# Blocks 3 and 4 of the tokens as a third pair with seven products of sums, on one core

## The chip, the core and the metric

The kernel runs on one core of a Trainium2 chip. Its engines are TensorE (PE, with weight loads as PEld), VectorE (DVE), ScalarE (ACT), GpSimd (POOL) and SyncE (SP), which here issues all the DMAs. The metric is device microseconds of one execution; the kernel before took a median of 988.34 us in three runs (987.86 to 989.14).

## The reference

Attention of 8 batches, 8 heads, 576 queries and head size 64, with keys and values averaged over groups of 8 positions (72 remain), and then a gated network with normalised rows on all 4608 tokens:

```python
k_p = k.reshape(B, H, Sp, pool, D).mean(axis=3)
v_p = v.reshape(B, H, Sp, pool, D).mean(axis=3)
scores = scale * np.matmul(q, k_p.transpose(0, 1, 3, 2))
attn = np.exp(scores - scores.max(-1)); attn = attn / (attn.sum(-1) + 1e-09)
x = np.matmul(attn, v_p)                      # to (4608, 512)
xn = x / np.sqrt(np.mean(x * x, -1) + 1e-06) * rms_g
g = xn @ w_gate                               # (512, 1536)
out = (g / (1 + np.exp(-g)) * (xn @ w_val)) @ w_out   # (1536, 512)
```

(Reductions keep their axis in the reference.) The weights arrive as float64 and are used as a high and a low fp32r half.

## The kernel before

**Blocks.** The 4608 tokens are nine blocks of 512. Each product of two fp32 operands is made as three fp32r matmuls (high by high, low by high, high by low). A block on its own ("plain") needs for each of the 12 column groups f of the hidden layer 12 matmuls for the gate and 12 for the value (`mm1`, L1016, into `psg`) and 12 for the output (`mm2`, L1050, into `po`): 432 in all. Blocks 0 to 4 are plain. Blocks 5 and 6, and blocks 7 and 8, are pairs: a pair is treated as a 2 by 2 block matrix that is multiplied with seven products instead of eight, in layer 1 (`product`, L852, into `pxy`, 12 x 7 x 6 = 504 matmuls) and in layer 2 (`product2`, L932, into `pf`, 7 x 6 x 6 = 252): 756 for two blocks.

**What a pair needs.** Sums of blocks of the weights: `w_whole` (high plus low, L712 on POOL or L714 on DVE, tile `wsum`), `w_sum` (L723, four sums for each f), `w_sumhi` (ACT, L728) and `w_sumlo` (L732, tile `wt`), for layer 2 `v_whole`, `v_sum`, `v_sumhi`, `v_sumlo` (L759, L763, L767). They are made while the plain blocks run and are stored to DRAM (`w_store`, `v_store`, and `w_blocks`, `v_blocks` for the unsummed parts), and in a pair each product loads its 256 KB back (`w_part` into `wp`, `f_part` into `ring`). Sums of the tokens (`p_sum`, `p_hi`, `p_lo`) are made just ahead of a pair. In a pair DVE and ACT combine the seven products (L1110 to L1119), and the sums of the hidden layer are formed on DVE and POOL (`f_sum`, `f_lo`, all through the helper `cut`, L272).

**Start.** The weights are split into halves by ACT, DVE and POOL (`w_abs` L298, `w_shift` L302, `w_low` L306, `w_sign` L310, `w_hi` L324, `w_lo` through L272) in the prelude and in block 0. The attention of batches 0 and 1 takes the `_` steps (`s_max`, `s_exp`, `s_inverse`, `s_norm`); that of batches 2 to 7 the `l_` steps. Attention has to be ahead of the block that uses its tokens: pair 5 and 6 uses batches 4 to 7.

**The order.** The string `ORDER` is a list of steps written by a planner and played back; nothing reorders it later. Each engine runs its instructions in that order and waits at each for its inputs. In a step's name the letters are the operation, the digits its indices (`mg1a` is the gate product of block 1, f = 10); figures behind `:` are PSUM banks and behind `/` buffer slots. SP's DMAs stand in one queue in the same order.

Of the kernel before, what the change touches and what calls it, by code (L numbers as in the profile page):

```python
# [57 lines left out]
_a0/0 _S10:24 _l7/0 _A030:6 _C032 _b0 _a2 _h1 _y01 _x00 _M100 _N010 _T010:5 _l4 _T012:7 _c0 _d0 _y00 _P00:3 _a4 _b4
_Z20 _M101 _D010 _x20 _A010:5 _h0 _E100 _y20 _E101 _C012 _W1 _A031:1 _A011 _A021:2 _x21 _Z31 _W0 _m000:7 _b2 _m010:4
_Z11 _c2 _x11 _X021 _d2 _R101 _y21 _m002 _R100 _x30 _c4 _d4 _m012 _k11 _Z10 _P01 _N101 _x10 _Z21 _h2 _l3/1 _y30 _N100  # L60
_T100:2/0 _y11 _x31 _a3/0 _b3 _q11 _Y011 _y10 _c3 _Z30 _P02 _P03 _m011 _W2 _l6 _a6 _m001 _h4 _V10/0 _p _r0 _m110:6
_y31 _m013 _b6 _T101 _d3 _T102:5 _s0 _c6 _l8 _a8 _B00:3 _d6 _Y031 _m003 _D100 _la _b8 _D101 _n _h6 _a7/1 _m100:1 _m112
_l9/1 _u0 _W4 _D102 _m102 _m111 _m101 _A100:5/1 _G0 _c8 _Y100 _K11/1 _d8 _S11:20 _m103 _W6 _F0 _i0/1 _M110 _h3 _aa _W3
_j0 _u1 _m113 _g2:3 _M111 _G1 _a9/0 _h8 _F1 _o0:6475 _W8 _i1/0 _E110 _L1 _b9 _E111 _c9 _d9 _e2:1 _h9 _W9 _ba _ca _da
_ha _b7 _e4:2 _c7 _q12 _k12 _o1 _d7 _lc _ac _Wa _u2 _bc _g3:3 _K12/1 _G2 _h7 _W7 _F2 _i2/1 _e3:0 _L2 _cc _dc _lb/1
_ld/0 _ab/0 _o2 _bb _u3 _le _g4:3 wd3 _ae _G3 _cb _R110 _N110 _R111 _v11 _ad/1 _F3 _i3/0 _be _hc _L3 _db _hb _o3
# [1097 lines left out]
```

## Time and profile before

| | |
|---|---|
| median of three runs | 988.34 us |
| the profiled execution | 985.33 us |
| its span, first to last instruction | 983.2 us |
| PE busy | 962.6 us (98%) |
| DVE / ACT / POOL busy | 665.9 / 477.1 / 446.8 us |
| moved by DMA | 178.37 MB, 181 GB/s |

The profiled execution is 3.0 us below the median and 2.1 us above its own span. A busy time is a union: an instruction counts until its end. A matmul's row gives the time from its start to its modelled end, and the next one starts well before that end, so the pace of PE is read from runs of matmuls in the chain and not from a mean. Borders between the blocks are the starts of their first `psg` or `pxy` matmul: block 0 at 40.1 us, then 166.8, 281.9, 397.1, 506.6 (block 4), 617.4 (first pair) and 780.4 (second pair).

### The profile page before, as it was taken

How to read it: one execution, taken by the hardware profiler on the slowest of the kernel's cores; microseconds unless marked ns; L12 is line 12 of the kernel's file. 1: busy time of each engine (PE TensorE's matmuls, PEld its weight loads, DVE VectorE, ACT ScalarE, POOL GpSimd, SP SyncE). 2: the span in 40 equal slices, each digit the busy share in tenths (PEclk: the TensorE clock that was granted, in tenths of full speed). 3: DMA queues.
4: the chain of work that ended last, by engine and by line, in shares of the span. 5: the costliest groups of instructions: out<-in, count | busy, mean ns of one | idle time of the engine just before them, and what ended most of it. 6: DMA issues, size and time to landing. Idle time of an engine off the chain costs nothing.

```text
span 983.2 us, 14009 instructions
## 1 busy us (share of the span) xinstructions
PE 962.6 (98%) x4778; PEld 768.7 (78%) x4778; DVE 665.9 (68%) x1043; ACT 477.1 (49%) x936; POOL 446.8 (45%) x535
## 2 busy tenths in 40 slices
PE   6899999999999999999999999999999999999997
PEld 6687878777877878778777778888787778888885
DVE  5997988666776576777686756665666885445343
ACT  6885776454554534743464254533434651222232
POOL 1688773223432543524453133323437762135567
PEclk7799999999999999999999999999999999999999
DMA  8546566466466444585435523776586565666546
GB/s 268 200 169 191 190 187 207 118 198 186 128 214 181 123 144 120 157 250 166 138 123 170 150 93 88 235 237 206 182 267 219 178 213 183 213 232 209 186 143 196
DMA packets 119542, 178.37 MB, mean 181 GB/s; under 512 B 10224, under 2 KB 67056, under 8 KB 118192
## 3 DMA queue, kind: packets, MB, share of 16 engines
q1 hardware_dynamic: 119472, 177.48, 57.4%
q8 instruction: 38, 0.62, 0.3%
q14 instruction: 32, 0.26, 0.1%
HBM read 121.21 MB, written 56.23 MB: 180 GB/s over the span
## 4 chain that ended last, share of the span: by engine, by line
PE 86%; DVE 6%; DMA 3%; ACT 2%; POOL 1%; issue 1%; SPq 0%; DVEq 0%; ACTq 0%; POOLq 0%
PE psg L1016 31%; PE pxy L852 23%; PE po L1050 16%; PE pf L932 9%; PE psx L521 3%; PE pss L439 3%; DMA v<-vN 2%; DVE wt L306 1%; DVE wt L310 1%; POOL fp L272 1%; DVE xl L272 1%; DMA ring<-vB 1%; DVE wt L302 1%; DMA ring<-vs 0%; POOL w L272 0%
## 5 line engine op out<-in xcount | busy, mean ns | idle before, releaser
L1016 PE MATMUL psg<-xh,w 128*128 128x512 f32 x928 | 289.4, 393 | 0.0
L852 PE MATMUL pxy<-xp,wp 128*128 128x512 f32 x1008 | 239.8, 390 | 1.5 <-ACT acc L591 1.0
L852 PEld LDWEIGHTS pxy<-xp,wp 128*128 128x128 f32 x1008 | 188.3, 188 | 43.6 <-issue 1.4
L1016 PEld LDWEIGHTS psg<-xh,w 128*128 128x128 f32 x928 | 172.0, 188 | 42.9 <-issue 4.1
L1016 PE MATMUL psg<-xl,w 128*128 128x512 f32 x464 | 181.0, 390 | 0.5 <-DVE xl L272 0.4
L272 POOL TENSOR_TENSOR hl<-act,hh 128x256 fp32r<-128x256 f32 x90 | 74.7, 850 | 160.0 <-ACT hh L1032 126.2
L932 PE MATMUL pf<-fp,ring 128*128 128x512 f32 x504 | 125.4, 391 | 1.5 <-DMA ring<-vB 1.0
L1050 PE MATMUL po<-w,hh 128*128 128x512 f32 x480 | 121.2, 390 | 0.0
L932 PEld LDWEIGHTS pf<-fp,ring 128*128 128x128 f32 x504 | 93.6, 188 | 24.2 <-issue 1.9
L1050 PEld LDWEIGHTS po<-w,hh 128*128 128x128 f32 x480 | 90.1, 188 | 19.0
L1016 PEld LDWEIGHTS psg<-xl,w 128*128 128x128 f32 x464 | 87.1, 188 | 19.9 <-DVE xl L272 1.4
L1028 DVE TENSOR_TENSOR act<-act,psg 128x512 f32<-128x512 f32 x60 | 41.0, 683 | 66.4 <-PE psg L1016 42.9
L272 POOL TENSOR_TENSOR w<-wt,w 128x256 fp32r<-128x256 f32 x68 | 72.3, 1090 | 13.7 <-ACT w L324 9.1
L1032 ACT CAST hh<-act 128x512 fp32r<-128x512 f32 x60 | 37.2, 619 | 74.5 <-DVE act L1028 48.4
L1050 PE MATMUL po<-w,hl 128*128 128x512 f32 x240 | 68.6, 397 | 1.4 <-POOL hl L272 1.4
L1050 PEld LDWEIGHTS po<-w,hl 128*128 128x128 f32 x240 | 43.9, 188 | 12.8 <-POOL hl L272 2.2
L272 POOL TENSOR_TENSOR fp<-fs,fp 128x256 fp32r<-128x256 f32 x54 | 41.2, 788 | 21.8 <-ACT fp L905 21.8
L272 POOL TENSOR_TENSOR fp<-act,fp 128x256 fp32r<-128x256 f32 x34 | 25.3, 764 | 50.5 <-ACT fp L905 49.1
L1023 ACT ACTIVATE act<-psg 128x512 f32<-128x512 f32 x48 | 28.6, 597 | 37.1 <-PE psg L1016 27.3
L1023 ACT ACT_TABLE_LOAD x26 | 33.4, 1283 | 22.3 <-PE psg L1016 15.6
L905 ACT CAST fp<-fs 128x512 fp32r<-128x512 f32 x36 | 21.7, 619 | 41.7 <-PE pf L932 24.9
L439 PEld LDWEIGHTS pss<-pk,q 64*128 64x128 f32 x560 | 33.4, 188 | 10.0 <-issue 7.3
(191 smaller groups left out, 1506.6 us busy)
## 6 DMA issues: line engine op xcount, KB each, us to landing
wp<-sum SPq DMA_DIRECT2D x96, 256.0 KB
wp<-blocks SPq DMA_DIRECT2D x72, 256.0 KB
blocks<-w SPq DMA_DIRECT2D x24, 512.0 KB
sum<-wt SPq DMA_DIRECT2D x48, 256.0 KB
ring<-vs SPq DMA_DIRECT2D x48, 256.0 KB
wx<-w SPq DMA_DIRECT2D x10, 1024.0 KB
v<-vN SPq DMA_DIRECT2D x32, 288.0 KB
ring<-vB SPq DMA_DIRECT2D x36, 256.0 KB
```

Of the source, the lines that this page charges most:

```text
L272: getattr(eng, op)(*(x[..., o:o + step] for x in (out, a, b)))
L302: nc.vector.tensor_scalar(u, u, 3, None, ALU.logical_shift_left)
L439: nc.tensor.matmul(s["ps", h][:, t * SP:(t + 1) * SP], s["q"][r, o:o + P], s["pk"][r, :], start=True, stop=True)
L521: nc.tensor.matmul(ps[r, :n], s["pv"][:, r], x, start=True, stop=True)
L852: nc.tensor.matmul(ps[:, :NB], w[:, a, c, :], x[:, b, c, :], start=j == 0 and not more, stop=j == len(todo) - 1, skip_group_check=more)
L905: nc.scalar.copy(y[:, 0], f_source(i, k, j))
L932: nc.tensor.matmul(ps[c], w[:, a, c * P:(c + 1) * P], x[:, b], start=j == 0 and n == 0 and not more, stop=j == HALF - 1 and n == 2, skip_g ...
L1016: nc.tensor.matmul(ps[:, :NB], w[:, c, cols], x[c], start=(j == 0), stop=(j == len(todo) - 1))
L1023: nc.scalar.activation(t, ps[:, :NB], AF.Silu)
L1028: nc.vector.tensor_mul(t, t, ps[:, :NB])
L1032: nc.scalar.copy(a, st["act", i, f])
L1050: nc.tensor.matmul(po[i][t], x[i, f][:, t * P:(t + 1) * P], w, start=(f == 0 and k == 0), stop=(f == NF - 1 and k == 2))
```

## The change

`FIRST`, the number of plain blocks, falls from 5 to 3, so that blocks 3 and 4 are a pair too. All the sums of the weights and the attention of batches 0 to 4 then have to be ready by the end of block 2. For the prelude there are three new steps: the second heads of batch 0 subtract the maximum on DVE (`s_sub`), take one exponential of 360 columns on ACT in place of five of 72 (`s_expall`), and sum and invert on DVE (`s_suminverse`), for which each row has a 73rd column of 1e-9. The factor 1/8 of the averaged values moves from the sum to the copies of `x`. `ORDER` is another string of 3315 steps (2990 before).

```diff
-FIRST = 5
+FIRST = 3
-            s["main"] = space1(NF - 1 - 2 * p, [P, 2 * S + 10 * SP], F32, f"main{p}")
+            s["main"] = space1(NF - 1 - 2 * p, [P, 2 * S + 10 * (SP + 1)], F32, f"main{p}")
+            nc.gpsimd.memset(rows(p)[:, :, SP:], 1e-9)
...
+    def s_sub(b, p, h):
+        s, n = st[b, p], len(OFFS2)
+        s["pr", h] = pr = s_rows(b, p, h)[:, :, :SP]
+        nc.vector.tensor_tensor(pr, s["ps", h][:, :n * SP].rearrange("p (t k) -> p t k", k=SP),
+                                s["mx"][:, h, :, None].broadcast_to([P, n, SP]), ALU.subtract)
+    def s_expall(b, p, h):
+        pr = st[b, p]["pr", h]
+        nc.scalar.activation(pr, pr, AF.Exp, scale=EXP_SCALE)
+    def s_suminverse(b, p, h):
+        sm = st[b, p]["sm"][:, h, :]
+        nc.vector.tensor_reduce(sm, s_rows(b, p, h), AX.X, ALU.add)
+        nc.vector.reciprocal(sm, sm)
...
-            copy(xraw[b][:, p, s["tok", u]], s["psx", u][:, :S // 2])
+            x, y = xraw[b][:, p, s["tok", u]], s["psx", u][:, :S // 2]
+        if eng is nc.scalar:
+            eng.mul(x, y, 1.0 / POOL)
...
-        if i < FIRST - 1:
+        if i < FIRST:
             t = sb1.tile([P, NC, n], F32, tag="q", name=f"tail{b}")
-        else:
-            t = space1(0, [P, NC, n], F32, f"tail{b}")
+            t = t[:, :2], t[:, 2:]
+        else:
+            t = sb1.tile([P, 2, n], F32, tag="q", name=f"tail{b}_0"), space2(NF - 1, [P, 2, n], F32, f"tail{b}_1")
...
-_l9/1 _u0 _W4 _D102 _m102 _m111 _m101 _A100:5/1 _G0 _c8 _Y100 _K11/1 _d8 _S11:20 _m103 _W6 _F0 _i0/1 _M110 _h3 _aa _W3
+_S11:27 _b9 _C102 _c9 _d9 _M110 _h9 _m102 _E110 _b8 _m110 _m112 _M111 _F0 _w9 _m101 _W6 _c8 _i0/1 _L0 Wf00 _d8 _lb/0
```

The engines' queues before and after show what the new order moves. First DVE in block 0, between the gate multiplications of f = 4 and f = 5 (`act0_4`, `act0_5`; `wt14`, `wt16` are weights being split, `wsum1` and `wt1_4` are sums for the pairs). Before:

```order
L1028 TENSOR_TENSOR act0_4_912<-act0_4_912,psg0_4_1_753 128x512
L306 SCALAR_TENSOR_TENSOR wt13_884<-wx13_838,wt13_884 128x512
L310 SCALAR_TENSOR_TENSOR wt13_884<-wx13_838,wt13_884 128x512
L306 SCALAR_TENSOR_TENSOR wt14_875<-wx7_857,wt14_875 128x1024
L310 SCALAR_TENSOR_TENSOR wt14_875<-wx7_857,wt14_875 128x1024
L404 TENSOR_REDUCE early_86<-pss1_2_0_953 128x5
L404 TENSOR_REDUCE early_86<-pss1_2_1_954 128x5
L990 TENSOR_TENSOR act0_5_1012<-xraw0_299,psg0_5_0_976 128x512
```

In the changed kernel the same stretch of DVE's queue, to the same multiplication (line numbers are those of the changed file):

```order
L1071 TENSOR_TENSOR act0_4_951<-act0_4_951,psg0_4_1_937 128x512
L326 SCALAR_TENSOR_TENSOR wt14_963<-wx7_934,wt14_963 128x1024
L330 SCALAR_TENSOR_TENSOR wt14_963<-wx7_934,wt14_963 128x1024
L419 TENSOR_REDUCE pv2_0_1007<-v2_0_1005 72x128
L757 TENSOR_TENSOR wsum2_1034<-w1_2_576 128x1024
L463 RECIPROCAL early_87<-early_87 128x5
L775 TENSOR_TENSOR wt1_4_1056<-wsum1_959,wt1_4_1056 128x256
L766 TENSOR_TENSOR wsum2_1034<-wsum2_1034 128x2x128
L775 TENSOR_TENSOR wt1_3_1027<-wsum1_959,wt1_3_1027 128x256
L322 TENSOR_SCALAR wt16_1071<-wt16_1071 128x1024
L766 TENSOR_TENSOR wsum2_1034<-wsum2_1034 128x2x128
L1033 TENSOR_TENSOR act0_5_1106<-xraw0_379,psg0_5_0_1043 128x512
```

The splitting of the weights stands where it stood, and the sums for the pairs, of which block 0 had none, now stand between them on DVE. Up to the gate multiplication of block 1, f = 0, DVE has 272 instructions where it had 217.

Second, SP's queue in the middle of the first pair, at the loads of layer 1 for f = 9 (`wp`), of layer 2 (`ring2`), and what belongs to attention (`k`, `q`, `v`, `rows`, `pt`). Before, in the pair of blocks 5 and 6:

```order
L841 DMA wp5_8_6_6887<-blocks8_5275 128x2x256
L920 DMA ring2_5999<-vB21_0_1958 128x512
L841 DMA wp5_9_3_6911<-sum9_3_4867 128x512
L480 DMA rows7_2_6932<-sq7_2_6736 32x3x256 x2
L480 DMA rows7_2_6932<-sq7_2_6736 32x3x320 x2
L485 DMA pt7_2_6937<-rows7_2_6932 72x1152
L841 DMA wp5_9_5_6939<-sum9_1_4921 128x512
L920 DMA ring2_5999<-vs1_2_3107 128x512
L841 DMA wp5_9_4_6951<-sum9_4_4852 128x512
```

In the changed kernel, in the pair of blocks 3 and 4:

```order
L884 DMA wp3_9_4_5440<-sum9_4_3080 128x512
L963 DMA ring2_3429<-vs0_2_1880 128x512
L884 DMA wp3_9_3_5463<-sum9_3_3023 128x512
L884 DMA wp3_10_3_5475<-sum10_3_3390 128x512
L390 DMA q6_3_5489<-qT 128x576
L884 DMA wp3_9_2_5491<-blocks9_3900 128x2x256
L401 DMA v6_3_5503<-vN 72x1024
L963 DMA ring2_3429<-vs1_2_2544 128x512
L884 DMA wp3_10_1_5527<-sum10_2_3291 128x512
L519 DMA rows6_2_5531<-sq6_2_5479 32x3x256 x2
L519 DMA rows6_2_5531<-sq6_2_5479 32x3x320 x2
```

The first pair now carries the attention of batches 5, 6 and the start of 7 in its loads, where before it had the end of batch 7 alone: from the pair's first product to the next pair's, SP issues 174 DMAs where it issued 139.

## Rows read from the trace of the kernel before

**Rows 1.** The page, busy us (share) by engine.

```profile
PE 962.6 (98%) x4778; PEld 768.7 (78%) x4778; DVE 665.9 (68%) x1043; ACT 477.1 (49%) x936; POOL 446.8 (45%) x535
```

**Rows 2.** Windows by block: us, busy PE, PEld, DVE, ACT, POOL, PEclk, DMA, GB/s.

```profile
40.10:166.80 126.70, 124.56 (x651) 100.21 (x650) 110.58 (x147) 91.54 (x196) 95.18 (x92) 0.98 0.56 181
166.80:281.90 115.10, 115.10 (x606) 90.92 (x605) 80.89 (x143) 58.28 (x102) 30.49 (x39) 1.00 0.54 164
617.40:780.40 163.00, 162.04 (x750) 130.29 (x748) 107.04 (x160) 70.02 (x114) 72.68 (x92) 1.00 0.68 217
780.40:983.20 202.80, 195.92 (x852) 158.70 (x852) 105.43 (x143) 61.67 (x105) 101.75 (x128) 1.00 0.62 197
```

**Rows 3.** Chain of waits in order of time: start us, us, what.

```profile
12.25 11.21 DMA v<-vN
78.02 4.27 POOL w L272 x4
...
198.41 8.16 PE psg L1016 x36
331.85 2.75 PE po L1050 x12
830.83 20.40 PE pxy L852 x90
```

**Rows 4.** Grouped instructions of DVE, shapes apart: busy us, mean ns, idle before.

```profile
L732 DVE TENSOR_TENSOR wt<-wsum,wt 128x256 fp32r<-128x256 f32 x30 | 16.5, 558 | 9.2 <-ACT wt L728 9.2
L723 DVE TENSOR_TENSOR wsum<-wsum 128x256 f32<-128x256 f32 x27 | 15.5, 576 | 0.9 <-POOL wsum L723 0.4
L714 DVE TENSOR_TENSOR wsum<-w 128x1024 f32<-128x1024 f32 x7 | 8.8, 1254 | 1.9 <-POOL acc L272 1.9
L272 DVE TENSOR_TENSOR hl<-act,hh 128x512 fp32r<-128x512 f32 x15 | 12.1, 810 | 5.1 <-ACT hh L1032 5.0
L272 DVE TENSOR_TENSOR w<-wt,w 128x1024 fp32r<-128x1024 f32 x1 | 1.2, 1218 | 0.0
L759 DVE TENSOR_TENSOR vsum<-vsum 128x256 f32<-128x256 f32 x16 | 7.8, 487 | 1.6 <-POOL vsum L272 1.3
L456 DVE TENSOR_TENSOR prob<-pss,mx 128x360 f32<-128x360 f32 x48 | 24.5, 524 | 0.7
L464 DVE TENSOR_REDUCE sm<-prob 128x5 f32<-128x365 f32 x48 | 25.0, 522 | 18.8 <-ACT prob L460 18.8
L469 DVE TENSOR_TENSOR prob<-prob,sm 128x360 f32<-128x360 f32 x40 | 25.3, 640 | 0.6
L503 DVE COPY own<-pst 72x512 f32<-72x512 f32 x7 | 4.6, 675 | 0.2 <-PE pst L497 0.2
```

**Rows 5.** Timeline near f = 9 of block 0, PE and DVE: start us, us.

```profile
136.65 0.39 PE L1016 MATMUL psg<-xl,w 128*128 128x512 f32 x1
...
143.65 0.69 DVE L310 SCALAR_TENSOR_TENSOR wt<-wx,wt 128x512 uint32<-128x512 uint32 x1
144.26 0.68 DVE L1028 TENSOR_TENSOR act<-act,psg 128x512 f32<-128x512 f32 x1
```

**Rows 6.** Instructions of tile wsum: ns min/median/max, first and last start.

```profile
L732 DVE TENSOR_TENSOR wt<-wsum,wt x30: 409/420/967, 183.6 to 691.9; 128x256 fp32r<-128x256 f32 x30
L723 DVE TENSOR_TENSOR wsum<-wsum x27: 384/419/950, 180.9 to 673.7; 128x256 f32<-128x256 f32 x27
```

**Rows 7.** Grouped instructions of ACT, shapes apart, columns as in Rows 4.

```profile
L460 ACT ACTIVATE prob<-prob 128x360 f32<-128x360 f32 x48 | 23.5, 504 | 27.9 <-DVE prob L456 27.7
L417 ACT ACTIVATE main<-pss,early 128x72 f32<-128x72 f32 x40 | 12.2, 321 | 0.3
```

**Rows 8.** Waits of PE from 617 to 983 us: in total, times, longest us.

```profile
PE pf L932 <- DMA ring<-vB: 1.0, 2, 0.7
```

**Rows 9.** Windows of the first 50 us, columns as in Rows 2.

```profile
0.00:25.00 25.00, 16.72 (x136) 15.35 (x136) 14.79 (x32) 16.49 (x89) 4.60 (x11) 0.80 0.87 266
25.00:50.00 25.00, 22.42 (x129) 15.94 (x130) 23.74 (x42) 21.12 (x67) 16.35 (x16) 0.78 0.59 209
```

More of the change, by code (lines that the diff above doesn't have):

```diff
@@ L58 @@
[L58 to L62, printed above, removed]
@@ new lines @@
+sm230/1 Nm230 vl13 Nm231 tr23/0 lv22/1 pv22/1 mo12 dp22/1 mg14:0 hi13/1 Lo13 ws51 me14 gt14 sc30:20 vl14 av221:1
+mx301/1 xd22 sb301 dm23 sq20 sq21/1 Jn21 ws52 Wt6/0 av220:3 Wf60 Wf61 xc221 lk31 dp23/1 xc220 sq22/1 ex301 Jn22
+mx300/0 pk31/0 mo13 hi14/1 lv30/1 sb300 Wf62 Lo14 wh61/0 Wl61 ws61 wh63/1 Wl63 ws63 wf63 mg15:0 gt15 sm301/0 nm301
+lk32 ex300 me15 pv30/1 av231:2 xc231 wh64/0 sm300/0 Nm300 Wl64 av230:1 mo14 wh62/1 Wl62 lv31/1 ws64 xc230 vl15 tr30/0
+hi15/0 Lo15 pk32/1 lq31 mg16:0 pv31/0 gt16 Zt10/1 ws62 Zf10 zh11/0 zl11 Zt11 Zf11 Zf12 me16:1 zh13/1 xd23 mo15 Zl13
@@ new lines @@
+lv40/0 gt23 vl23 pv40/1 me24:0 rt31 hi23/1 mg24:1 kt2 sm400/1 wsa3 Nm400 Lo23 tr40/0 Zf30 wsa4 zh31/1 Zf31 lq41
+sc41:23 mx411/1 Zl31 sb411 dm40 zs31 ft300 Zf32 zh33/0 Zl33 zs33 mo23 gt24 vl24 ex411 me25 Zf33 zh34/1 zl34 mx410/0
+lk43 hi24/0 Lo24 sb410 dp40/0 sm411/0 Wtb/0 Wfb0 mg25 pk43/0 ex410 zh32/0 zl32 sm410/1 zs34 whb1/1 Nm411 Nm410 tr41/1
+mo24 gt25 Wlb1 vl25 hi25/1 Lo25 Wfb1 zs32 mg26:1 Wfb2 av400:2/1 xc400 lq42 sc42:03 me26:2 gt26 rc31 whb2/0 mx420/1
+sb420 wsb1 ex420 whb3/1 dm41 rs31 vl26 Wlb3 mx421/1 sb421 mo25 av401:1 ft301 sm420/0 xd40 hi26/0 Lo26 ex421 sm421/0
@@ new lines @@
+ft364 pm364 dp70/1 av700:6/0 xc700 Fl510 Fl365 va52 ft365 av701:5 pm365 rl540/0 xc701 qh31 qh30 sw52 vb52 pr530:6
+pr531:7 pr540 cp53 pr533:1 vb51 u253 u353 fh502/5 rl541/3 rl542/1 Fs511 fh501/6 cp54 rl535/6 c253 rl532/5 pr535:7
+lv71/0 pr532 rc61 rl543/7 pr543:0 sm710/0 rl545/4 v253 pr541:4 u254 u354 xd70 pr542 rl550/2 ft500 rl536/6 pr536
+sm711/1 lq72 v153 ft501 pr550:0 pm500:54 cp55 Nm710 sw53 vb53 fs512 Fl501 rl552/3 Fl502 rl551/1 sa53 Nm711 tr71/1
+pr552 oh30 va53 Fs513 pr551:7 fh503/3 u255 rl553/6 rl544/0 pr545:1 pr544:3 c254 sw54 v254 rl555/7 rl546/1 pr555:6
@@ new lines @@
+pr5b0:3 pr5b1:0 Fl533 sa59 va59 rl5a6/3 pm532 ft523 ft533 v25a pr5a6 fh523/6 Fl523 pm533 sw5a vb5a cp5b Fs544 u25b
+Fs534 dp73/0 av730:2 fh542/8 Fl542 fh534/5 v15a rl5b6/1 av731:1 xd73 Fs563 pm523 rl5b2/6 fh541/7 Fl541 va5a xc731
+xc730 sq73/0 Jn73 Fl534 rl5b3/0 fh524/6 pr5b3:1 u35b pr5b4:0 ft534 sh7/0 sl7 rl5b5/2 Fl524 c25b ft543 sw5b pr5b5:2
+v25b vb5b fs535 rm71:1 ft542 rm70 pm524 rt71 ft540 pr5b2 fh540/6 rc71 rt70 sa5b pm534 rc70 Fl540 ft541 Fs545 pr5b6
+fh544/5 pm540:30 Fl544 v15b va5b pm541 fh525/6 pm542 rs70 pm543 ft544 pm544 rl710/0 rs71 fh535/8 rl702/2 ys73/10 yh70
@@ new lines @@
+pr750:3 sw72 v272 pr726 v172 rl741/1 rl754/5 va72 rl736/6 fh702/4 Fl702 fh711/8 rl751/7 pr736 cp74 pr741:2 v173 sa73
+va73 fh703/7 ft702 vb72 Fs712 u274 cp75 rl761/3 ft710 rl753/0 pr751:0 u275 pr761:1 oh51 Fl710 Fl703 pr742 rl743/2
+pr743:2 u374 fh712/5 ft701 pm701 rl744/7 pr744:7 rl746/2 c274 rl745/3 sa74 sw73 vb73 rl760/4 Fs713 pr753:2 sw74 u375
+pr754:6 c275 sw75 pr745:7 rl752/1 pr752 sa75 oh50 v274 pr746 rl755/6 pr755:0 pr760 cp76 rl763/3 vb74 rl756/1 Fl711
+rl771/0 v275 vb75 pr756 v174 va74 ft711 fh704/6 Fl704 pr771:7 pm702 rl770/5 pr770:3 v175 pr763:0 u276 u376 va75
@@ new lines @@
+rl7b3/2 rl7b4/6 ft724 pr7a6 fh723/3 pm733 ft743 Fl723 vb7a Fs734 ft734 Fs763 pm723 fh750/7 rl7b2/7 v17a sa7a va7a
+pr7b3:2 fh724/3 Fl724 pr7b1:1 fh734/5 ft742 Fl734 pr7b0:3 cp7b u27b pm724 rl7b6/0 rl7b5/5 ft740 fs743 pr7b2 pm734
+ft741 Fs744 sa7b fh743/3 Fl743 u37b pr7b4:3 c27b pm740:12 Fs764 ft744 fh742/5 Fl742 pr7b5 pm741 ft745 v27b sw7b vb7b
+fs735 pr7b6 pm742 pm743 fh744/4 Fl744 pm744 Fs745 fh735/6 Fl735 v17b va7b fh725/5 Fl725 ft725 pm725 fh745/3 ft735
+pm735 qe70/1 Fl745 fh752/5 Fl750 qc71 ft752 pm745 Qd71 ft750 fh753/3 fl753 ft751 qc70 Fl752 pm750:74 pm751 fh754/4
@@ L248, in body @@
     gcol = const.tile([P, NC], F32, name="gcol")
+    gmean = const.tile([P, NC], F32, name="gmean")
     eps = const.tile([P, 1], F32, name="eps")
@@ L254, in body @@
     tiny = const.tile([P, 1], F32, name="tiny")
-    nc.vector.memset(tiny, POOL * 1e-9)
+    nc.vector.memset(tiny, 1e-9)
     early = const.tile([P, NP, 2, 2, 8], F32, name="early")
@@ L342, in main, with rows @@
         if "main" not in s:
-            s["main"] = space1(NF - 1 - 2 * p, [P, 2 * S + 10 * SP], F32, f"main{p}")
+            s["main"] = space1(NF - 1 - 2 * p, [P, 2 * S + 10 * (SP + 1)], F32, f"main{p}")
+            nc.gpsimd.memset(rows(p)[:, :, SP:], 1e-9)
         return s["main"]
+    def rows(p):
+        return st[0, p]["main"][:, 2 * S:].rearrange("p (g k) -> p g k", k=SP + 1)
     def own(p):
@@ L404, in s_max, with s_rows @@
         nc.vector.tensor_reduce(mx, s["ps", h][:, :n * SP].rearrange("p (t k) -> p t k", k=SP), AX.X, ALU.max)
+    def s_rows(b, p, h):
+        n = len(OFFS2)
+        return (rows(p) if b == 0 else prob[:, :, :SP + 1])[:, h * n:(h + 1) * n, :]
     def s_exp(b, p, h):
         s, n = st[b, p], len(OFFS2)
-        if b == 0:
-            pr = main(p)[:, 2 * S:].rearrange("p (g k) -> p g k", k=SP)
-        else:
-            pr = prob[:, :, :SP]
-        s["pr", h] = pr = pr[:, h * n:(h + 1) * n, :]
+        s["pr", h] = pr = s_rows(b, p, h)[:, :, :SP]
         mx, sm = s["mx"][:, h, :], s["sm"][:, h, :]
@@ L417, in s_exp @@
             nc.scalar.activation(pr[:, t, :], s["ps", h][:, t * SP:(t + 1) * SP], AF.Exp, scale=EXP_SCALE,
-                                 bias=s["mx"][:, h, t:t + 1], accum_out=s["sm"][:, h, t:t + 1])
-        nc.scalar.activation(sm, sm, AF.Identity, scale=float(POOL), bias=tiny)
+                                 bias=mx[:, t:t + 1], accum_out=sm[:, t:t + 1])
+        nc.scalar.activation(sm, sm, AF.Identity, bias=tiny)
+    def s_sub(b, p, h):
+        s, n = st[b, p], len(OFFS2)
+        s["pr", h] = pr = s_rows(b, p, h)[:, :, :SP]
+        nc.vector.tensor_tensor(pr, s["ps", h][:, :n * SP].rearrange("p (t k) -> p t k", k=SP),
[7 more added lines that the diff above has]
+        nc.vector.reciprocal(sm, sm)
     def s_inverse(b, p, h):
@@ L535, in l_xlast, with s_xcopy @@
                                 ALU.mult)
-    def s_xcopy(b, p, u, copy):
+    def s_xcopy(b, p, u, eng):
         s = st[b, p]
         if b == 0:
-            copy(xraw[b][:, p, NB:], s["psx", u][:, NB - S // 2:S // 2])
+            x, y = xraw[b][:, p, NB:], s["psx", u][:, NB - S // 2:S // 2]
         else:
-            copy(xraw[b][:, p, s["tok", u]], s["psx", u][:, :S // 2])
+            x, y = xraw[b][:, p, s["tok", u]], s["psx", u][:, :S // 2]
+        if eng is nc.scalar:
+            eng.mul(x, y, 1.0 / POOL)
+        else:
+            eng.tensor_scalar(x, y, 1.0 / POOL, None, ALU.mult)
     def s_xsq(p, u):
         s = st[0, p]
-        nc.scalar.activation(own(p)[:, 2 * S:3 * S][:, s["tok", u]], s["psx", u][:, :S // 2], AF.Square)
+        nc.scalar.activation(own(p)[:, 2 * S:3 * S][:, s["tok", u]], s["psx", u][:, :S // 2], AF.Square, scale=1.0 / POOL)
     root = {}
@@ L973, in first_hi @@
         d = (slice(0, S // 2), slice(S // 2, NB))[u]
-        nc.scalar.mul(XH[0][c][:, d], st[0, c]["psx", u][:, :d.stop - d.start], gcol[:, c:c + 1])
+        nc.scalar.mul(XH[0][c][:, d], st[0, c]["psx", u][:, :d.stop - d.start], gmean[:, c:c + 1])
     def first_lo(c, u):
@@ L979, in first_lo @@
         d = (slice(0, S // 2), slice(S // 2, NB))[u]
-        nc.vector.scalar_tensor_tensor(XL[0][c][:, d], st[0, c]["psx", u][:, :d.stop - d.start], gcol[:, c:c + 1],
+        nc.vector.scalar_tensor_tensor(XL[0][c][:, d], st[0, c]["psx", u][:, :d.stop - d.start], gmean[:, c:c + 1],
                                        XH[0][c][:, d].bitcast(F32), ALU.mult, ALU.subtract)
```

298 lines of the change are left out of this document (146 added, 152 removed).

## The prediction

> **What bounds the kernel now.** I read the busy times first: PE is busy for 98% of the span, DVE for 68%, ACT and POOL for under half [rows 1]. Next the windows by block: from 40.1 us on PE is busy for 124.56 of 126.70 us in block 0, for all of block 1 and for 162.04 of 163.00 us in the first pair; only the last window, which holds the end of the program, has a loss of 7 us [rows 2]. So a matmul less is time less, as long as the other engines keep ahead of PE. Then the chain of waits: up to 23.5 us it lies on loads of `v`, from there through DVE, ACT and POOL, and after a run of POOL at 78.02 us on matmuls nearly throughout [rows 3]. The first 80 us are therefore not PE's, and DVE is busy for 23.74 of 25 us between 25 and 50 us [rows 9]. Block 0 is also where DVE has least in hand: 110.58 of 126.70 us busy, against 80.89 of 115.10 in block 1 [rows 2]. The question is what the new order puts on DVE there.
>
> **Matmuls removed.** Two plain blocks are 2 x 432 = 864 matmuls of 512 columns, a pair is 756, so 108 go. One costs 8.16 / 36 = 0.2267 us in layer 1 of a plain block, 2.75 / 12 = 0.229 in its layer 2 and 20.40 / 90 = 0.2267 in a pair [rows 3]: 108 x 0.2267 = 24.5 us, all in stretches without gaps. The clock is 1.00 there [rows 2], the upper of the two levels, 2.4 GHz. Attention's matmuls are the same in number.
>
> **DVE in block 0.** Up to the gate multiplication of block 1, f = 0, DVE gets 272 instructions for 217. The difference by kinds, with the mean of the nearest row [rows 4]:
> 15 weight sums at 0.576 and 15 of their low halves at 0.558 make 17.0 us; 4 sums of high and low at 1.254 make 5.0; 7 low halves of split weights that leave POOL, five at 0.810 (the row of the same shape) and two at 1.218, make 6.5; 2 more low halves of the hidden layer 1.6; 7 small steps for layer 2's sums at 0.487, 3.4; the second heads of batch 0, four times a subtraction (0.524) and a sum (0.522; their reciprocals replace others), 4.2; a part of batch 2's attention that comes earlier, one maximum and two sums at 0.522, a subtraction at 0.524 and a scaling at 0.640, 2.7; and 7 copies of 0.675 that go to ACT take off 4.7. Together 35.7 us by durations. Back to back an instruction of 0.69 us lets the next start after 0.61 [rows 5], so that I count 35.7 x 0.88 = 31.5 us.
> DVE's idle time in the window is 126.70 - 110.58 = 16.1 us [rows 2]. If all of it is filled, DVE comes to the end of block 0 some 15.4 us later than it did. How late it may come without PE waiting is seen at f = 9: PE ended the products at 137.04 us, DVE began the multiplication that frees their bank at 144.26 [rows 5], and PE had no wait there. These 7.2 us are the slack, and the rest, 8.2 us, becomes a wait of PE in block 0 or at the start of block 1. What is queued behind DVE's sums is that multiplication, behind it ACT's cast to `hh`, POOL's `hl`, and PE's output matmuls; and also the `xl` parts with which block 1 begins. I take 8 us.
> The bounds: a weight sum alone takes 0.42 us (the median, both kinds), at worst 0.95 to 0.97 [rows 6]. At 0.42 the thirty cost 4.4 us less by durations, 3.9 of DVE's time, and PE waits 4.3 us; and if what PE needs always stands ahead of the sums in DVE's queue, it waits 0. At 0.96 they cost 11.8 more, or 10.4, and PE waits 18.6; if moreover none of the 16.1 us of idle time can be filled, because DVE meets the same waits on ACT and POOL again, it is 34.7. I stay at the mean since POOL, with fewer weights to split, should be in the way no more often than it was.
> *The Trainium skill*, "SBUF — State Buffer", section "Who interferes with whom", says that a DVE instruction with two SBUF inputs contends with a GpSimd instruction that reads SBUF, and that whichever is first holds the shared ports for its whole length while the other waits. The trace agrees with two kinds of duration for one shape, 0.42 and 0.95 [rows 6]. By that rule a POOL that is never idle in block 0 (95.18 of 126.70 us busy, [rows 2]) would put all thirty at the upper duration, which is the 18.6 us above and speaks against the change.
>
> **Block 1 and later.** Between the same multiplications of blocks 1 and 2 DVE gets 183 instructions for 139; 44 at about 0.57 x 0.88 are 22 us, and 34 were free [rows 2]: no charge. If block 0's delay were larger, though, only these 12 us could catch it up.
>
> **The added pair's stretch.** From its first product to that of the next pair PE has 84 + 25 product steps of six matmuls (148 us) and attention and an output step, some 168 us in all. The first pair before moved 217 x 163.00 = 35.4 MB [rows 2]. In the new order SP issues 18 more loads of `k`, `q` and `v`, four more rounds through `rows` and five more loads of `pt`, less six of `ring`: about 7.5 MB, so 43 MB in 168 us or 255 GB/s. The most in any window is 266 GB/s, with the DMA engines busy for 0.87 [rows 9], so it fits, without much to spare. PE lost 1.0 us in two waits on these loads before [rows 8]; I put 2 us on the new pair. Bounds 0 and 14 (27 of the 109 steps, one in four, waiting 0.5). DVE had 56 us free in the old pair's window [rows 2], more than the two batches of attention that come into it.
>
> **The prelude.** Each second head gives ACT one exponential of 0.504 us for five of 0.321 [rows 7], four times 1.1 us. I cost this gain at nothing: the load of `v` that ends at 23.46 us and DVE behind it hide it [rows 3]. Were ACT the path, it would be 4.4 us; if the loads of `v`, which stand behind more weights now, come later, it is a loss of 2. The new tail's two tiles, the 73rd columns and the factor 1/8 change no path.
>
> **The sum.** -24.5 + 8 + 2 = -14.5 us, against the profiled execution's own 985.33: 970.8. The median of the runs is 3.0 above that execution, so 973.8: I predict 974 us. The forecast's own range, 968 to 982, has a chance of 0.50.
>
> **Rivals.**
> *All of it is hidden*, 0.27. The order was laid out as a whole, and what PE needs may stand early enough on DVE. For it speaks that PE has waited for DVE almost nowhere; against it, that the idle time in block 0 is half of what comes. 988.3 - 24.5 = 964 us.
> *Transfers bind the third pair*, 0.08. The 14 us above in place of 2: 986 us. For it: 255 GB/s asked of a stretch where no loss can hide. Against it: the loads can run ahead, and the two pairs before lived with 0.68 and 0.62 [rows 2].
> *DVE's queue in block 0 costs more than the matmuls give*, 0.12, slower. Every sum meets POOL, and the idle time can't be filled: PE waits the 34.7 us above; -24.5 + 34.7 + 2 = +12, so 1000 us. It decides from 22.5 us of waits of PE on. For it: block 0 already begins with DVE, ACT and POOL on the chain [rows 3], and DVE's extra 31.5 us are twice its idle time. Against it: POOL gets less work, and sums come after what is due in most places of the queue.
> The remaining 0.03 is a clock that falls: it was granted 0.80 and 0.78 over the first two windows, in which PE had gaps [rows 9]; if PE's new waits keep the lower level, 1.2 GHz, for another 8 us, that is 4 us more, or 978, inside the range.
>
> **Chances.** Under 0.2% (2 us) this kernel's measurement can't tell from no change. The forecast, the clock case and the first rival are faster by more; of the transfers' 0.08 half lies between 986 and 990. Faster 0.84, same 0.04, slower 0.12. The range that leaves out the slower rival and the end of the transfers' case is 962 to 988.
>
> **What would show it.** PE's matmuls: 4670 where 4778 were, and pairs from about 400 us. Block 0's window longer by about 8 us, DVE busy there for over 95%, and waits of PE on `act`, `hl` or `xl` of 1 to 4 us between 90 and 175 us; the sums' mean near 0.57. In the third pair about 250 GB/s and waits on `wp` or `ring` of some 2 us. I am wrong in the middle of the sum if block 0 keeps its 126.7 us, and wrong in the whole if the first product starts later than 440 us.

## The result

The changed kernel took a median of 977.43 us (976.88 to 978.55, four runs) beside 988.18 us for the kernel before (987.86 to 989.14); the ratio is 0.9891, with a 95% interval of 0.9874 to 0.9908. Forecast were 974 us and a gain of 14.3; measured is a gain of 10.8. Run again beside the experiments, the ratio was 0.9884 (0.9859 to 0.9909).

The profiled execution took 976.88 us and its span 975.1, against 985.33 and 983.2 before. Busy times of the changed kernel, which answer to [rows 1]:

```profile
PE 947.5 (97%) x4670; PEld 752.2 (77%) x4670; DVE 704.2 (72%) x1134; ACT 492.9 (51%) x929; POOL 490.4 (50%) x618
```

There are 108 matmuls fewer, as counted. The windows by block (columns as in [rows 2]; block 0, block 1, then the new pair and the next):

```profile
38.60:180.90 142.30, 135.36 (x682) 106.06 (x681) 127.47 (x190) 98.39 (x215) 78.80 (x81) 0.94 0.63 207
180.90:299.00 118.10, 118.10 (x633) 92.33 (x632) 100.46 (x194) 64.10 (x120) 28.08 (x36) 1.00 0.66 205
...
409.00:584.30 175.30, 173.56 (x859) 135.56 (x858) 137.34 (x221) 92.39 (x146) 94.90 (x123) 1.00 0.80 247
584.30:779.90 195.60, 193.80 (x912) 155.16 (x911) 129.56 (x197) 88.21 (x139) 113.77 (x148) 1.00 0.69 216
```

Attention has moved between the blocks, so lengths alone mislead. Give each matmul its undisturbed pace (0.2267 us for 512 columns, those of attention by their own), and what a stretch took beyond that is lost, by my estimate:

| from its first product | before: us, lost | after: us, lost |
|---|---|---|
| start to block 0 | 40.1 | 38.6 |
| block 0 | 126.7, 7.3 | 142.3, 20.1 |
| block 1 | 115.1, 2.4 | 118.1, 3.0 |
| block 2 | 115.2, 2.5 | 110.0, 1.8 |
| blocks 3 and 4 | 220.3, 4.5 | 175.3, 6.6 |
| blocks 5 and 6 | 163.0, 3.2 | 195.6, 5.3 |
| blocks 7 and 8 to the end | 202.8, 4.8 | 195.2, 5.0 |

The losses grew by 17.1 us, 12.8 of them in block 0, 2.1 in each of the first two pairs. The 12.8 have more than one source. PE's idle time in block 0 grew by 4.8 us, to 142.30 - 135.36 = 6.9 from 2.1 [rows 2]. The mean granted clock of the block fell from 0.98 to 0.94: below full clock are 0.06 x 142.3 = 8.5 us now and 0.02 x 126.7 = 2.5 before, so some 6 us by this estimate. About 2 are not placed. Where PE waited in block 0 (in total, times, longest us):

```profile
PE pst L536 <- POOL prob L468: 2.3, 2, 2.0
PE po L1093 <- ACT prob L441: 1.5, 1, 1.5
PE psg L1059 <- DVE prob L495: 1.0, 1, 1.0
PE po L1093 <- POOL hl L292: 0.9, 1, 0.9
PE psx L560 <- ACT own L590: 0.8, 1, 0.8
PE po L1093 <- DVE hl L292: 0.4, 1, 0.4
```

Only 1.4 of these 6.9 us name DVE. The longest shows how DVE is behind others all the same. Timeline near it (start us, us), POOL, DVE, ACT and PE:

```profile
108.87 5.32 POOL L292 TENSOR_TENSOR w<-wt,w 128x256 fp32r<-128x256 f32 x4 [3.03 <-ACT w L344]
114.15 0.90 POOL L766 TENSOR_TENSOR wsum<-wsum 128x256 f32<-128x256 f32 x1
115.01 1.71 POOL L468 TENSOR_TENSOR prob<-prob,early 128x360 f32<-128x360 f32 x2
...
97.65 2.69 DVE L766 TENSOR_TENSOR wsum<-wsum 128x256 f32<-128x256 f32 x3
...
107.64 0.39 DVE L775 TENSOR_TENSOR wt<-wsum,wt 128x256 fp32r<-128x256 f32 x1
113.52 0.95 DVE L775 TENSOR_TENSOR wt<-wsum,wt 128x256 fp32r<-128x256 f32 x1
...
102.51 0.62 ACT L1075 CAST hh<-act 128x512 fp32r<-128x512 f32 x1 [1.40 <-DVE act L1071]
...
115.85 0.63 PE L536 MATMUL pst<-ident,prob 128*72 128x128 f32 x4 [1.96 <-POOL prob L468]
```

PE's transposes wait for `prob`, which stands on POOL behind a weight's low halves and a sum; before the low halves POOL had stood idle for 3.03 us on ACT's cast of that weight (L344, at 107.75 us). ACT came to this cast late: it had been at work without a gap since 102.51 us, and before that it had stood idle for 1.40 us on DVE's gate multiplication (L1071, at 101.75 us), which stood in a queue without a gap behind, among others, three sums. The rows also show both durations of a sum: 0.39 us while POOL stood still, 0.95 while it ran.

### The profile page after: what moved, and what is told of

It is laid out like the page before. It is cut to its first block, busy times and chain, and to the rows that moved or that the text cites. A ratio compares the mean times of both kernels' runs of the same rounds, so it can differ in the third digit from the quotient of the medians.

```text
span 975.1 us, 14181 instructions
## 1 busy us (share of the span) xinstructions
PE 947.5 (97%) x4670; PEld 752.2 (77%) x4670; DVE 704.2 (72%) x1134; ACT 492.9 (51%) x929; POOL 490.4 (50%) x618
## 4 chain that ended last, share of the span: by engine, by line
PE 76%; DMA 5%; DVE 5%; POOL 5%; ACT 3%; issue 2%; SPq 1%; DVEq 0%; ACTq 0%; POOLq 0%
PE pxy L895 30%; PE psg L1059 15%; PE pf L975 15%; PE po L1093 7%; PE psx L560 3%; PE pss L478 3%; POOL w L292 2%; DMA pt<-rows 1%; DMA ring<-vs 1%; POOL xp L292 1%; POOL hl L292 1%; DMA ring<-vB 1%; DVE wt L326 1%; PE psr L652 1%; DVE wt L330 1%
## 5 line engine op out<-in xcount | busy, mean ns | idle before, releaser
L895 PE MATMUL pxy<-xp,wp 128*128 128x512 f32 x1512 | 361.1, 391 | 1.5 <-ACT o L1104 0.7
L895 PEld LDWEIGHTS pxy<-xp,wp 128*128 128x128 f32 x1512 | 282.3, 188 | 65.3 <-issue 2.5
L975 PE MATMUL pf<-fp,ring 128*128 128x512 f32 x756 | 189.8, 393 | 3.1 <-DMA ring<-vB 1.6
L1059 PE MATMUL psg<-xh,w 128*128 128x512 f32 x544 | 171.2, 396 | 1.4 <-DVE prob L495 1.0
L975 PEld LDWEIGHTS pf<-fp,ring 128*128 128x128 f32 x756 | 139.6, 188 | 39.6 <-DMA ring<-vs 3.9
L1059 PEld LDWEIGHTS psg<-xh,w 128*128 128x128 f32 x544 | 101.2, 189 | 26.5 <-DVE prob L495 1.4
L1059 PE MATMUL psg<-xl,w 128*128 128x512 f32 x272 | 106.7, 392 | 0.0
L292 POOL TENSOR_TENSOR fp<-fs,fp 128x256 fp32r<-128x256 f32 x108 | 81.1, 778 | 41.7 <-ACT fp L948 37.9
L1093 PE MATMUL po<-w,hh 128*128 128x512 f32 x288 | 72.9, 390 | 0.0
L292 POOL TENSOR_TENSOR fp<-hb,fp 128x256 fp32r<-128x256 f32 x68 | 54.5, 828 | 13.9 <-ACT fp L948 13.9
```

Source lines behind the costliest of these rows:

```text
L292: getattr(eng, op)(*(x[..., o:o + step] for x in (out, a, b)))
L895: nc.tensor.matmul(ps[:, :NB], w[:, a, c, :], x[:, b, c, :], start=j == 0 and not more, stop=j == len(todo) - 1, skip_group_check=more)
L975: nc.tensor.matmul(ps[c], w[:, a, c * P:(c + 1) * P], x[:, b], start=j == 0 and n == 0 and not more, stop=j == HALF - 1 and n == 2, skip_g ...
L1059: nc.tensor.matmul(ps[:, :NB], w[:, c, cols], x[c], start=(j == 0), stop=(j == len(todo) - 1))
L1093: nc.tensor.matmul(po[i][t], x[i, f][:, t * P:(t + 1) * P], w, start=(f == 0 and k == 0), stop=(f == NF - 1 and k == 2))
```

## Experiments

All are changes to the changed kernel; line numbers can shift by a few. Ratios are to the kernel before, run beside each group; its medians were 990.03 us beside a0 to e3, 988.78 beside e4 to e7 and 988.31 beside e8 to e11. e1 and e8 leave out part of the work; all the others compute everything.

| run | median us | ratio (95%) | block 0, us |
|---|---|---|---|
| a0 the changed kernel | 978.32 | 0.9884 (0.9859 to 0.9909) | 140.9 |
| e1 narrow sums | 972.28 | 0.9812 (0.9789 to 0.9835) | 133.9 |
| e2 sums on POOL | 990.15 | 1.0012 (0.9988 to 1.0035) | 155.4 |
| e3 filled gaps | 980.44 | 0.9901 (0.9880 to 0.9923) | 146.2 |
| e4 sums after block 0 | 1052.3 | 1.0641 (1.0612 to 1.0670) | 135.3 |
| e5 some sums later | 1048.98 | 1.0610 (1.0583 to 1.0637) | 143.4 |
| e6 old heads | 982.05 | 0.9932 (0.9912 to 0.9953) | 142.6 |
| e7 more transfers | 1010.81 | 1.0239 (1.0212 to 1.0266) | 138.6 |
| e8 no sums | 968.88 | 0.9806 (0.9778 to 0.9834) | 133.3 |
| e9 two more heads | 978.04 | 0.9898 (0.9874 to 0.9921) | 138.8 |
| e10 all of batch 1 | 987.01 | 0.9995 (0.9977 to 1.0013) | 149.5 |
| e11 first heads | 980.57 | 0.9921 (0.9896 to 0.9946) | 139.2 |

**a0, the changed kernel again.**

> The changed kernel once more, beside the same runs of the kernel before as the three that follow. All theories: 0.989 of before, 976 to 978.5 us. What it tells is how much block 0 differs from one execution to the next: the first profile had its 142.3 us with 6.9 us of waits of PE and a granted clock of 0.94.

As expected; block 0 lost 18.7 us here, with the same waits to 0.3 us.

**e1, narrow sums.**

```diff
 def w_sum(f, k, eng):
-    eng.tensor_sub(place(f, y), place(f, a), place(f, b))
+    n = 8 if f < 5 and eng is nc.vector else P
+    eng.tensor_sub(*(place(f, x)[..., :n] for x in (y, a, b)))
```

(and the same width in `w_sumlo`).

> The 27 weight sums that DVE makes in block 0 (and four more in block 1) are cut to 8 of 128 columns of each half, and the stores of those sums send the high half twice, so the sums of f = 0 to 4 are not computed. DVE is relieved of 27 x (0.64 - 0.1) = 14 to 15 us in block 0. Theory 1 (the sums on DVE are what block 0 waits for): most of the 12.8 us that block 0 lost comes back, 8 to 12 us, so 965 to 969 us. Rival (the loss is the clock, which falls in the gaps of the start, and waits on ACT and POOL that DVE's sums do not cause): under 3 us, 974 to 977 us.

0.9812 against 0.9884: 0.0072, or 7 us (6.0 by the medians). Block 0 of e1 (window, then the waits that are left there of those above):

```profile
41.00:174.80 133.80, 129.44 (x682) 101.58 (x681) 121.22 (x189) 98.27 (x215) 76.70 (x80) 0.98 0.67 218
```

```profile
PE po L1096 <- ACT prob L441: 1.2, 1, 1.2
PE po L1096 <- POOL hl L292: 0.9, 1, 0.9
PE pst L536 <- POOL prob L468: 0.9, 1, 0.9
```

The wait on POOL's `prob` falls from 2.3 to 0.9 though nothing was taken from POOL, and ACT's cast to `hh`, which had waited for DVE, now waits for PE:

```profile
99.69 0.62 ACT L1078 CAST hh<-act 128x512 fp32r<-128x512 f32 x1 [0.92 <-PE po L1096]
```

Theory 1 holds, with a smaller size than expected. One reason is that DVE's sums in block 0 still took 10.8 of their 17.8 us: a narrow one with no POOL instruction beside it took 0.16 to 0.18 us, but one beside POOL up to 0.84. And the shorter block 0 of this trace is not all theirs: PE's idle time in it is 4.4 us where a0 had 6.4, while the granted clock was 0.98 where a0 had 0.95, and between 40 and 60 us it was already higher (0.84, under e3), before the first narrow sum at 65.3 us. The times carry the result: all five, 970.09 to 972.63 us, lie below all six of a0, 976.19 to 981.35. Their mean clocks average 0.984 and 0.981, so up to 0.003 x 975 = 3 of the 7 us, by an estimate, can be the clock's; whether the sums move the clock no run shows.

**e8, no sums.** `w_whole`, `w_sum`, `w_sumhi` and `w_sumlo` return at once for f < 4.

> All sums of layer 1 for f = 0 to 3 are left out on all engines (25 sums and four whole sums on DVE, seven sums on POOL, 16 casts on ACT); the stores send a part of the high weights in their place, in the same number and size. Of the 12.8 us that block 0 lost, the narrowed sums gave back some 7.5. Theory 1, full form (the sums with what they cost on ACT and POOL are all of the loss): block 0 falls to 130 us or less and the time to 964 to 968 us. Rival (the last 4 to 5 us come from the order of the rest, attention and the start, and not from the sums): block 0 stays at 132 to 135 us, 969 to 972 us.

0.9806: 7.7 us below a0, 0.6 more than e1, whose interval it shares. In block 0 it brought DVE's busy time from e1's 121.2 us to 106.4, and with the sums went their work on POOL and ACT and SP's waits for them; what all this gives beyond e1 is within the noise. PE's waits in block 0 are all but gone (1.1 us), and its idle time is 133.30 - 131.92 = 1.4 us where the changed kernel had 6.9 and a0 6.4. So 5 to 5.5 of the 7.7 us are PE's waits. Yet the block kept 133.3 us: the rival holds for the rest.

**e2, the sums on POOL.** `Wf00` becomes `wf00` and so on, 27 steps.

> The same 27 sums are made on POOL in the same places of the order, 27 x 0.75 = 20 us more on POOL (79 of 142 us busy in block 0), some 16 us less on DVE. Theory 1 (DVE's queue): 2 to 6 us faster than the changed kernel, 971 to 975 us. Rival (what PE waits for in block 0 comes from POOL, behind the splitting of weights, so the sums were rightly put on DVE): slower than the changed kernel, 980 to 992 us, with waits of PE on POOL's hl and prob.

12 us slower, the rival's outcome, with its waits (the longest two):

```profile
PE po L1093 <- POOL hl L292: 6.0, 3, 3.8
PE psx L560 <- ACT xraw L583: 3.1, 1, 3.1
```

POOL was busy for 100.6 of 155.4 us only, but `hl` stands in its queue behind the sums. The clock fell as well: between 60 and 180 us it was 0.93 where the changed kernel had 0.99, which is 0.06 x 120 = 7 us by an estimate. DVE is the lesser evil.

**e10, all of batch 1; e9, two of its heads; e11, the first heads of batch 0.** In the order each `_E` step becomes `_U` and `_O`, each `_R` an `_I`.

> All eight heads of batch 1 in the new form: 8 x 1.5 us less on ACT, 8 x 0.87 = 7 us more on DVE, six of the eight in block 0. If what PE waits for in block 0 is ACT (the wait of 1.5 us on prob): 973 to 976 us. Theory 1 (DVE's queue): 979 to 984 us.

> The two heads of batch 1 that are made in the start (p = 0) get the new form too: one exponential in place of five on ACT (1.1 us each and the step that negates the maximum less), a subtraction and a sum more on DVE (0.87 us each). The run with the old heads cost 4.4 us, so ACT is on the path of the start. If it still is: 1 to 3 us faster than the changed kernel, 975 to 977 us. Rival (the path is DVE's by now, 21.8 of 25 us busy between 25 and 50 us): 978 to 980 us.

> The four first heads of batch 0 in the new form too: 4 x 1.5 us less on ACT, 3.5 us more on DVE in the first 20 us, where DVE was busy for 17.5 of 25 us and ACT for 14.5. If ACT is the path from the start on: 974 to 977 us. Rival (DVE): 979 to 982 us.

Some seven microseconds more on DVE and twelve less on ACT made e10 slower than a0 by 0.0111, 11 us, worse than theory 1 had it, and here the waits name DVE (L449 is the new subtraction):

```profile
PE po L1094 <- DVE prob L449: 4.8, 1, 4.8
PE psg L1060 <- DVE prob L449: 3.9, 2, 3.2
```

PE's idle time in block 0 was 149.50 - 135.38 = 14.1 us, at the changed kernel's clock (0.94). With e1 and e8 this is the same term with both signs: DVE's queue binds in block 0. The new subtractions are links of attention itself, though, so e10 alone doesn't tell a fuller queue from a longer chain. e9 and e11 can't be told from the changed kernel; both lie where the rival had them.

**e6, old heads.** For the second heads of batch 0 the steps `_U`, `_O`, `_I` become `_E` and `_R`.

> The second heads of batch 0 are made as before (five exponentials that subtract the maximum and sum, in place of a subtraction, one exponential and a sum), in the same places of the order. As predicted (the gain on ACT is hidden, cost nothing): the same as the changed kernel within 2 us, 976 to 980 us. Rival 1 (ACT is the path of the start): 980 to 983 us. Rival 2 (the 4.2 us that the new form gives to DVE are what holds up the first 60 us): 972 to 975 us.

0.9932 against 0.9884 is 4.7 us (3.7 by the medians): rival 1's outcome, and not what I predicted. The first product came at 44.9 us, where the eight profiled executions with the new start unchanged (the first one, a0, e1, e2, e4, e5, e7 and e8) had it at 37.7 to 41.0. The waits of PE in the start name ACT's exponentials of the old form (L441):

```profile
PE pss L478 <- ACT main L441: 3.4, 1, 3.4
PE pst L536 <- ACT main L441: 3.0, 1, 3.0
```

**e3, filled gaps.** `_z5:0` ahead of `_T031`, `_z5:4` ahead of `_A020`, `_z3:4` ahead of `_A031`.

> Thirteen matmuls of the identity that nobody reads are put into PE's queue ahead of three steps of the start for which PE waits (five before the transposes at 29.8 us, five before the product at 34.1, three before the one at 44.7; 0.34 us each, 4.4 us). Clock theory: with the gaps filled the clock does not fall to 0.5 at 36 to 41 us and at 46 to 56 us, which is about 6 us of the time; 3 to 5 us come back, 972 to 974 us. Rival (DVE, ACT and POOL bound the first 80 us anyway): the clock rises and PE waits longer on the others, 976 to 979 us.

No gain, and the clock did not rise (0.64 between 40 and 60 us), so the test is weak and settles neither: the third filling waited itself for 1.8 us on its bank. Windows from 40 to 60 us (us, PE busy, granted clock, DMA share, GB/s) of before, changed, a0, e3, e7 and e1, the last five with the same order of the other work in this stretch:

```profile
40.00:60.00 20.00, 19.27 (x104) 0.85 0.35 130
```

```profile
40.00:60.00 20.00, 19.18 (x87) 0.68 0.42 145
```

```profile
40.00:60.00 20.00, 19.25 (x82) 0.61 0.55 196
```

```profile
40.00:60.00 20.00, 18.17 (x81) 0.64 0.45 154
```

```profile
40.00:60.00 20.00, 19.66 (x120) 0.87 0.44 157
```

```profile
40.00:60.00 20.00, 19.43 (x119) 0.84 0.52 178
```

PE is busy for over 18 of 20 us in all of them, and the clock between its two levels (1.2 and 2.4 GHz, 0.50 and 1.00) makes the difference: 81 to 120 matmuls. It differs as much between executions of one order (0.61, 0.68, 0.87 in a0, the changed kernel and e7) as between the kernels. Block 0 ended at 181.7, 180.9 and 177.7 us in these three, so it is worth some 3 to 4 us to an execution. What sets it stays open.

**e7, more transfers.**

```diff
         nc.sync.dma_start(w.bitcast(F32), src)
+        if i == 3:
+            nc.sync.dma_start(dram.tile([P, 2, 2, P], F32, tag=f"copy{f}_{k}", ...), src)
```

> Each of the 84 loads of layer-1 weights of the third pair is followed on SP by a copy of the same 256 KB to a place in DRAM that nobody reads, so some 43 MB become at least 65 MB in the 175 us of that pair. If the transfers there are well hidden, as predicted (2 us of waits): the pair grows by 0 to 4 us, 976 to 982 us. Rival (247 GB/s is close to what the queue gives beside the rest): the pair grows by 10 us or more, 988 us or more, with waits on wp and ring.

The rival's size. The third pair took 204.8 us, and there

```profile
405.80:610.60 204.80, 181.19 (x859) 138.36 (x858) 136.91 (x221) 92.25 (x146) 92.61 (x122) 0.98 0.96 318
```

with PE's longest waits

```profile
PE pxy L897 <- DMA wp<-blocks: 9.8, 6, 3.4
PE psx L560 <- DMA pt<-rows: 5.4, 4, 3.0
```

At 318 GB/s the DMA engines are busy for 0.96: that is the ceiling of this mix (copies within DRAM included). The changed kernel asks for 247 there. If the ceiling without the copies is the same, which no run shows, its own 43.3 MB (247 x 175.3) would take 136 us: an estimate by which the transfers are hidden with about a fifth in hand.

**e4, sums after block 0, and e5, some of them.** Only steps of the order and their buffer slots move.

> The order is changed and nothing else: all the steps of the layer-1 sums (whole, sum, high, low, store) of f = 0 to 4 that stood in block 0 come behind its last step and are made in blocks 1 and 2; the last of the sums stand where they stood. DVE loses 27 sums (17.9 us) and four sums of high and low (5.7 us) in block 0, POOL 10 instructions, ACT 18 casts, SP 18 stores; blocks 1 and 2 of the changed kernel had 17.6 and 19.9 us of DVE free. Theory 1 (the sums on DVE are what block 0 waits for, and they are cheap elsewhere): block 0 shrinks by 7 to 10 us, the rest stays, 967 to 971 us. Rival (the sums only carry their waits into blocks 1 and 2, or reach the third pair's loads too late): 975 us or more, with waits of PE on wp.

> As the run above, but 11 of the 27 sums of DVE stay in the last part of block 0. Theory 1: between the two, 969 to 973 us; what counts is that the sums leave the stretch up to 120 us where the weights are split. Rival: 975 us or more.

Block 0 of e4 lost 13.2 us where the changed kernel's lost 20.1 and 18.7, which is theory 1 a third time, and the cleanest: at the changed kernel's clock (0.94) PE's idle time in the block is 135.30 - 133.08 = 2.2 us instead of 6.9. But "cheap elsewhere" was wrong: block 1 grew from 118.1 to 184.7 us. Waits in its first 184 us, of SP and of ACT:

```profile
SPq L779 <- DVE wt L775: 70.3, 21, 8.5
```

```profile
ACT wt L771 <- DMA sum<-wt: 42.8, 15, 6.9
```

A sum is a chain over DVE, ACT, DVE and a store through one of two buffers. Pressed together, the next sum's cast waits for the last one's store, and SP, which has one queue, waits for the sum with attention's loads behind it: PE then waits on `pt`, `q` and `hl`. DVE was busy for 118.1 of 184.7 us. That free time on DVE had no use without free slots.

e5 is the rival's outcome too, and its block 0 (143.4 us) did not shrink as theory 1 had it. One wait of PE did that:

```profile
PE psb L676 <- DVE r L667: 6.1, 1, 6.1
```

`r` stood in DVE's queue behind the low half of a sum, at which DVE stood idle until its cast came:

```profile
167.05 0.43 DVE L775 TENSOR_TENSOR wt<-wsum,wt 128x256 fp32r<-128x256 f32 x1 [6.55 <-ACT wt L771]
```

So a sum can hold up PE through DVE's queue also when DVE has little to do.

None of the runs that compute everything beats the changed kernel; e9 equals it.

## Why the prediction was right, and where it was not

**The matmuls** went as predicted: 108 fewer, at the same pace (48 of `pxy` in 10.88 us, 0.2267 each, against [rows 3]):

```profile
834.80 10.88 PE pxy L895 x48
```

**DVE's queue in block 0**, +8 us: without the sums 7 (e1) to 7.7 us (e8) come back, of which 5 to 5.5 are PE's waits. The size is near; the way to it was not right, and that it came near is partly luck. I let the new work fill DVE's 16.1 idle us first. It did not: 142.30 - 127.47 = 14.8 us stayed idle and DVE was busy for 90%, not over 95%. And DVE's work there grew by 16.9 us, not 31.5. The two errors cancel: 31.5 less 16.1 is 15.4, and 16.9 less the 1.3 that were filled is 15.6. The work grew less for two reasons. My count ran from the start of the program to the gate multiplication at 190.5 us, so that of the 55 instructions only 43 are in the window (190 for 147); the 4.2 us of the second heads, for one, lie before it. And the splitting became cheaper, 55.4 us for 63 instructions in block 0 instead of 68.7 for 66. The waits that I had announced, on `act`, `hl` or `xl`, came mostly on `prob`, and the window grew by 15.6 us where I had announced 8, with 6 us of the clock and moved attention in it. Grouped DVE instructions in block 0 (columns as in [rows 4]), before:

```profile
L310 DVE SCALAR_TENSOR_TENSOR wt<-wx,wt 128x1024 uint32<-128x1024 uint32 x10 | 15.7, 1572 | 0.2
L310 DVE SCALAR_TENSOR_TENSOR wt<-wx,wt 128x512 uint32<-128x512 uint32 x13 | 12.5, 965 | 0.3
```

and after:

```profile
L330 DVE SCALAR_TENSOR_TENSOR wt<-wx,wt 128x1024 uint32<-128x1024 uint32 x9 | 12.4, 1374 | 0.1
L766 DVE TENSOR_TENSOR wsum<-wsum 128x256 f32<-128x256 f32 x14 | 10.5, 748 | 0.8 <-POOL wsum L766 0.6
L330 DVE SCALAR_TENSOR_TENSOR wt<-wx,wt 128x512 uint32<-128x512 uint32 x12 | 9.0, 752 | 0.1
L775 DVE TENSOR_TENSOR wt<-wsum,wt 128x256 fp32r<-128x256 f32 x14 | 7.4, 526 | 0.4 <-ACT wt L771 0.3
```

POOL was busy for 78.80 us of the longer block instead of 95.18, and the splits took 1.37 us instead of 1.57 and 0.75 instead of 0.97. The weight sums in block 0 took 0.748 rather than the 0.576 of the mean, their low halves 0.526 rather than 0.558: 17.8 us for 28 where I had 17.0 for thirty. The rule of the Trainium skill that I weighed ("SBUF — State Buffer", "Who interferes with whom") is right in kind: of the 80 sums of 256 columns on DVE, the 50 with no POOL instruction beside them took 0.417 us on average and at most 0.427, the other 30 averaged 0.741 and reached 1.03. But only about half of block 0's 28 met POOL long enough to be lengthened, where the 18.6 us took all thirty.

**The clock**, to which I gave 0.03 and 4 us more, took more of block 0 in the profiled run than PE's waits did: some 6 us by the estimate above, and 0.17 x 20 = 3.4 of them between 40 and 60 us (0.68 where it was 0.85). I had it follow from PE's new waits, and these are not the whole reason: e8 had hardly a wait left in block 0, and 0.95 over the block. Right behind the longest wait, between 115 and 122 us, the clock was 0.76 in the profiled run and 1.00 in a0, which had that wait too. And between 40 and 60 us it differs from execution to execution, so that only part of it is the change's.

**The prelude**, costed at nothing: the new heads are worth 4 to 5 us (e6), and 4.4 was the price I had named for the case that ACT is the path. My reason against it, the load of `v` on the chain, came from the old start [rows 3]. In the changed kernel's start the chain (start us, us) goes over ACT, the new exponential first (L453), and then DVE:

```profile
26.62 0.41 ACT main L453
27.02 0.52 ACT w L344
...
31.33 1.82 DVE wt L326 x2
```

The start as a whole gained less: the first product came at 38.6 us (37.7 to 41.0 in the eight executions named under e6) against 40.1. Where the rest of it went no run shows.

**The third pair**, +2: losses there rose by 2.1 us over the two plain blocks, but PE's waits on DMA, which I had meant, were 1.0 of them (`wp` 0.5, `ring` 0.3, `pt` 0.2). Not foreseen: 2.1 us more in the next pair, which now has more of attention to do (912 matmuls where it had 750). Whether attention is the cause was not tested.

The sum for the profiled runs: attention that left the start adds 1.5 to the blocks by their paces, and the start is 1.5 shorter, so -24.5 + 1.5 + 17.1 - 1.5 = -7.4; with 0.7 that is left over at the end of the program this makes the span's 8.1. The medians differ by 10.8 because the profiled execution of before (985.33) lay below all its other runs (987.86 to 989.14). So part of how near 974 came to 977.43 is luck as well: from profiled execution to profiled execution I had 970.8, and 976.88 was measured.

**The rivals.** All hidden: false, since e1 and e8 got 7 us back by leaving sums out. Transfers bind: false, but e7 puts the ceiling only 29% above what the pair asks for (318 over 247). DVE's queue above 22.5 us: false by far, though e2 and e10, which are not far from this order, lose the whole gain.

## What to carry to other kernels

An engine that is 10% idle can be the bound: price work added to an in-order queue by what stands behind it, and expect idle slots between dependent instructions to stay empty. When work moves from one engine to another, re-price every instruction that shared memory with it, not the moved ones only. Before moving work to a stage with free time, count the buffers and the queue slots its chain needs there.

## Not expected of the hardware

Executions of one kernel spread with the granted clock: beside e8 to e11 the kernel before took 984.45 to 987.28 us in eight executions with a mean clock of 0.984 to 0.988, and 988.31 to 991.27 in nine with 0.980 to 0.984. A clock of 0.007 more is 0.007 x 983 = 7 us, which is the size of the spread. And 247 GB/s with the DMA engines at 0.80 let PE wait for 1 us in 175, while with 318 GB/s at 0.96 the same pair took 30 us longer.
